# Local attention, a sine-and-cosine mixing layer and a gated layer on one core: a residual added by accumulating transfers, a shorter float64 conversion, a rounding moved to ScalarE

## The chip, the cores and the metric

The kernel runs on one core of a Trainium2 chip. The metric is the time of one execution in device microseconds (us). Besides plain times there is a profile: one execution recorded by the hardware profiler. TensorE multiplies matrices from SBUF into PSUM; VectorE (DVE) and ScalarE (ACT) do elementwise work; GpSimd (POOL) is almost unused; SyncE (SP) issues transfers. Every engine works through its own queue in order.

## The reference

Three layers follow one another on 4 batches of 768 tokens and 512 channels.

```python
# 1. local attention, 8 heads of 64: a chunk of 32 queries sees 8 memory keys,
#    16 keys to the left, its own 32 and 8 to the right
out[:, :, c0:c1] = softmax(q_c @ k_full.T / 8) @ v_full
x = out.transpose(0, 2, 1, 3).reshape(4, 768, 512)
# 2. mixing
theta = x @ w_theta
zr, zi = x * cos(theta), x * sin(theta)
u = x + einsum('ts,bsd->btd', w_tok_r, zr) + einsum('ts,bsd->btd', w_tok_i, zi)
x = u + maximum(u @ w_ch, 0)
# 3. gated layer
h = gelu_tanh(x @ w_in);  a, v = h[..., :512], h[..., 512:]
v_n = (v - mean(v)) / sqrt(var(v) + 1e-6) * g_ln
x = x + (a * (w_sg @ v_n + b_sg)) @ w_out
```

The weights w_theta, w_tok_r, w_tok_i, w_ch, w_in and w_out arrive as float64, all else as float32.

## The kernel before

Each factor of a large product is split into a rounded part `hi` and a remainder `lo`, and a product is taken as hi*hi + hi*lo + lo*hi, three matmuls where one would do.

Attention works in 24 blocks of 128 tokens (6 for each batch). Each block has four steps: `att_s` (scores, maximum, exponential), `att_t` (TensorE transposes the probabilities), `att_v` (values, division) and `att_x` (TensorE transposes the result, and `split` makes `xhi`, `xlo`). Each block loads its `q`, `ka` and `va` on SP's queue.

The mixing layer works in 48 units, one for each turn of the loop over `it`. A unit holds one block of 128 source tokens: for batch 0 all 512 channels and one half of the target tokens (12 units), for batches 1 to 3 256 channels and both halves (36 units). `theta(n)` multiplies for the angle (in turns, since 1/2pi is folded into w_theta), takes off the nearest whole number by adding and subtracting MAGIC = 1.5 * 2^23, and makes sine and cosine on ScalarE; `z_split(n)` splits x*cos and x*sin. `mix_group(n, g)` adds 6 matmuls of 128x384 into one of four accumulators in PSUM; it is called with g = 0 to 3 in each unit. In the last unit of six the accumulators are complete: two VectorE additions put xhi and xlo on top (lines 388, 389; `u` has two buffers), and SP stores 192 KB into `u_dram` (line 390). This end of four groups comes eight times. `theta` and `z_split` run two units ahead of `mix_group`.

The 4 pieces of w_theta and the 12 of w_tok are converted from float64 while the first units run. `Weights.load` brings a piece to SBUF as pairs of 32-bit words; `bits` makes the float32 with truncated mantissa from the upper word (one ScalarE pass, three VectorE passes; the third masks out the exponent); then `convert` (10 pieces of w_tok, all of w_ch and w_in) multiplies the lower word by that power of two, subtracts hi and adds: three more VectorE passes. `convert_pe` (4 pieces of w_theta, 2 of w_tok) leaves these last sums to TensorE, as three matmuls with an identity, and ScalarE copies the result. `conv_out` does the same for the 4 pieces of w_out.

After the mixing layer, `chan` takes u from `u_dram` for u + max(u @ w_ch, 0), and the gated layer follows, batch by batch.

The framework puts a semaphore wait wherever an instruction needs another's result or its buffer.

Of the kernel before, what the change touches and what calls it, by code (L numbers as in the profile page):

```python
# [6 lines left out]
F32 = mybir.dt.float32  # L7
# [13 lines left out]
NBLK = S // 128  # L21
# [11 lines left out]
def net_kernel(tc, qt, kw, vw, ident, w_theta, w_tok, w_ch, w_in, w_sg, w_out, g_ln, b_sg, out):  # L33
# [33 lines left out]
    id_th = stg.tile([128, 128], F32, name="id_th", bufs=1)  # L67
    id_r = stg.tile([128, 128], F32R, name="id_r", bufs=1)
    id_neg = stg.tile([128, 128], F32R, name="id_neg", bufs=1)
# [44 lines left out]

    class Weights:
# [28 lines left out]
        def bits(self, raw, n, scale, mag="act", rem="dve"):  # L144

            words = raw[:, 0:2 * n].rearrange("p (n t) -> p n t", t=2)
            low, high = words[:, :, 0], words[:, :, 1]
            h = self.pool.tile([128, self.n], I32, tag="cvh", name="cvh", bufs=self.ncv)[:, 0:n]
            m = self.pool.tile([128, self.n], I32, tag="cvm", name="cvm", bufs=self.ncm)[:, 0:n]
            nc.scalar.activation(  # L150
                out=h.bitcast(F32), in_=high.bitcast(F32), func=AF.Copy, scale=REBIAS
            )
            nc.vector.tensor_scalar(
                out=h, in0=h, scalar1=3, scalar2=None, op0=ALU.logical_shift_left
            )
            nc.vector.scalar_tensor_tensor(  # L156
                out=h, in0=high, scalar=-0x80000000, in1=h,
                op0=ALU.bitwise_and, op1=ALU.bitwise_or,
            )
            nc.vector.tensor_scalar(  # L160
                out=m, in0=h, scalar1=-0x800000, scalar2=None, op0=ALU.bitwise_and
            )
            return high, low, h, m

        def convert_pe(self, j, scale=None, bank=None):

            if j >= len(self.pieces):
                return
            _, hi, lo = self.pieces[j]
            raw, n, _ = self.raw.pop(j)  # L170
            one = 1.0 if scale is None else scale
            high, low, h, m = self.bits(raw, n, scale)

            w, rest = h.bitcast(F32), lo
            nc.scalar.activation(out=hi, in_=w, func=AF.Copy, scale=one)
            nc.vector.scalar_tensor_tensor(
                out=rest, in0=low.bitcast(U32), scalar=one * 2.0 ** -52, in1=m.bitcast(F32),
                op0=ALU.mult, op1=ALU.mult,
            )
            step = n if n <= 512 else n // 2  # L180
            for c in range(0, n, step):
                cv = (bank or th_tile)()[:, 0:step]
                c = slice(c, c + step)
                nc.tensor.matmul(
                    out=cv, lhsT=id_sb if scale is None else id_th, rhs=w[:, c],
                    start=True, stop=False,
                )
                nc.tensor.matmul(out=cv, lhsT=id_neg, rhs=hi[:, c], start=False, stop=False)
                nc.tensor.matmul(out=cv, lhsT=id_r, rhs=rest[:, c], start=False, stop=True)
                nc.scalar.activation(out=lo[:, c], in_=cv, func=AF.Copy)  # L190

        def convert(self, j, mag="act", rem="dve", sub="dve", add="dve"):
            if j >= len(self.pieces):
                return
            eng = {"dve": nc.vector, "pool": nc.gpsimd}
            _, hi, lo = self.pieces[j]
            raw, n, wide = self.raw.pop(j)
            if not wide:
                split(hi, lo, raw[:, 0:n].bitcast(F32), eng[sub])
                return  # L200
            high, low, h, m = self.bits(raw, n, None)
            w, rest = h.bitcast(F32), m.bitcast(F32)
            nc.scalar.activation(out=hi, in_=w, func=AF.Copy)
            nc.vector.scalar_tensor_tensor(
                out=rest, in0=low.bitcast(U32), scalar=2.0 ** -52, in1=rest,
                op0=ALU.mult, op1=ALU.mult,
            )
            eng[sub].tensor_tensor(out=w, in0=w, in1=r32(hi), op=ALU.subtract)  # L208
            eng[add].tensor_tensor(out=lo, in0=w, in1=rest, op=ALU.add)
# [69 lines left out]
    def att_x(i):  # L279
# [8 lines left out]
        split(xhi[:, :, 128 * s:128 * s + 128], xlo[:, :, 128 * s:128 * s + 128], tp3)  # L288


# [10 lines left out]
    def theta(n):  # L301
# [16 lines left out]
        else:  # L318
# [3 lines left out]
        nc.vector.tensor_scalar(  # L322
            out=t, in0=th, scalar1=MAGIC, scalar2=MAGIC, op0=ALU.add, op1=ALU.subtract
        )
# [39 lines left out]
    def mix_group(n, g):  # L364
# [18 lines left out]
        if last:  # L383
            _, xhi, xlo = sets[b % 2]
            dt = d0 + d2
            tt = slice(TC * th, TC * th + TC)
# [217 lines left out]
    def conv_out(k):  # L604
# [5 lines left out]
        nc.scalar.activation(  # L610
# [454 lines left out]
```

## Time and profile before

| | us |
|---|---|
| median of 3 runs | 746.72 |
| lowest and highest of them | 746.16 and 748.55 |
| the profiled execution | 749.29 |
| its span (first to last instruction) | 747.5 |
| TensorE busy | 723.0 |
| VectorE busy | 524.9 |
| ScalarE busy | 318.9 |
| GpSimd busy | 0.3 |

"Busy" is the time in which an engine has at least one instruction at work. Matmuls are pipelined, so a busy TensorE is not one at its peak: what it can do at best is read from the distance between the starts of matmuls that wait for nothing. Recorded durations of neighbours on one engine overlap a little. "PEclk" is the share of TensorE's full clock that was granted.

### The profile page before, as it was taken

To read this page: it belongs to the slowest core of one execution; us is meant where nothing else is said; L and a number is where in the kernel's file an instruction comes from. 1 tells how busy PE (TensorE), PEld (TensorE's weight loads), DVE (VectorE), ACT (ScalarE), POOL (GpSimd) and SP (SyncE) were. 2 spreads that over 40 slices of the span, in tenths; PEclk is the share of its full clock that TensorE was granted. 3 is DMA by queue.
4 is the path that set the end of the run, shared out by engine and by line. 5 is a ranking of instruction groups with operands and counts; after the bars stand their busy time and mean duration, and the time that the engine had idled before them with its cause. 6 is when DMAs were issued, how large, how long until landed. Compare 5 with 4: busy or idle time off the path is not lost.

```text
span 747.5 us, 16071 instructions
## 1 busy us (share of the span) xinstructions
PE 723.0 (97%) x6920; PEld 671.3 (90%) x6920; DVE 524.9 (70%) x980; ACT 318.9 (43%) x482; POOL 0.3 (0%) x6
## 2 busy tenths in 40 slices
PE   5998999999999999999999999999999999999997
PEld 2676788899999999999999998999899989998997
DVE  3999898856656575699539976977446744774375
ACT  4767553645455445463314416722342233224320
POOL 0000000000000000000000000000000000000000
PEclk9998999999999999999999999999999999999999
DMA  9575465522333331062049837002200310030002
GB/s 349 197 275 197 147 226 158 202 73 86 131 108 121 101 134 53 23 233 61 12 150 345 317 136 255 1 0 91 80 1 0 111 59 1 1 116 11 1 1 85
DMA packets 33047, 86.89 MB, mean 116 GB/s; under 512 B 3792, under 2 KB 16208, under 8 KB 32976
## 3 DMA queue, kind: packets, MB, share of 16 engines
q1 hardware_dynamic: 32976, 85.87, 33.3%
q8 instruction: 54, 0.88, 0.5%
q14 instruction: 17, 0.14, 0.1%
HBM read 66.98 MB, written 18.87 MB: 115 GB/s over the span
## 4 chain that ended last, share of the span: by engine, by line
PE 78%; DVE 14%; ACT 4%; DMA 2%; issue 1%; SPq 0%; DVEq 0%; ACTq 0%
PE acc L378 16%; PE acc L664 13%; PE acc L540 9%; PE acc L578 9%; PE acc L432 9%; PE th L311 7%; PE att L702 6%; PE att L234 3%; DVE z L336 1%; DVE cvh L156 1%; PE att L258 1%; PE att L284 1%; PE th L702 1%; PE acc L702 1%; DVE cvh L208 1%
## 5 line engine op out<-in xcount | busy, mean ns | idle before, releaser
L378 PE MATMUL acc<-tok,slot 128*128 128x384 f32 x552 | 116.8, 342 | 2.5 <-ACT slot L348 2.5
L378 PE MATMUL acc<-slot 128*128 128x384 f32 x552 | 115.5, 340 | 0.0
L378 PEld LDWEIGHTS acc<-tok,slot 128*128 128x128 f32 x552 | 94.6, 188 | 4.6 <-ACT slot L348 2.8
L378 PEld LDWEIGHTS acc<-slot 128*128 128x128 f32 x552 | 95.6, 188 | 1.7
L664 PE MATMUL acc<-sg_hi,vhi_all 128*128 128x384 f32 x192 | 64.5, 336 | 0.0
L664 PE MATMUL acc<-sg_lo,vhi_all 128*128 128x384 f32 x192 | 64.5, 336 | 0.0
L664 PE MATMUL acc<-sg_hi,vlo_all 128*128 128x384 f32 x192 | 64.3, 336 | 0.0
L311 PE MATMUL th<-th_hi,xhi 128*128 128x256 f32 (+1 forms) x168 | 52.8, 314 | 1.3 <-ACT xhi L112 1.1
L311 PE MATMUL th<-th_hi,xlo 128*128 128x256 f32 (+1 forms) x168 | 51.4, 306 | 0.6 <-DVE xlo L113 0.6
L311 PE MATMUL th<-th_lo,xhi 128*128 128x256 f32 (+1 forms) x168 | 50.6, 301 | 0.0
L112 ACT ACTIVATE gop<-gv_all 128x384 fp32r<-128x384 f32 (+1 forms) x28 | 15.9, 571 | 76.7 <-DVE gv_all L673 51.6
L669 DVE SCALAR_TENSOR_TENSOR gv_all<-acc,g_col,b_bc 128x384 f32<-128x384 f32 x32 | 19.6, 615 | 41.0 <-PE acc L664 41.0
L578 PE MATMUL acc<-x3lo,in_hi 128*128 128x384 f32 x128 | 43.1, 337 | 0.0
L578 PE MATMUL acc<-x3hi,in_hi 128*128 128x384 f32 x128 | 43.1, 337 | 0.0
L578 PE MATMUL acc<-x3hi,in_lo 128*128 128x384 f32 x128 | 43.1, 337 | 0.0
L432 PE MATMUL acc<-uhi,ch_hi 128*128 128x384 f32 x128 | 42.8, 335 | 0.0
L432 PE MATMUL acc<-ulo,ch_hi 128*128 128x384 f32 x128 | 42.8, 335 | 0.0
L432 PE MATMUL acc<-uhi,ch_lo 128*128 128x384 f32 x128 | 42.8, 334 | 0.0
L547 DVE BATCH_NORM_STATS2 bn<-gv_all 128x6 f32<-128x512 f32 x24 | 16.7, 694 | 33.7 <-ACT gv_all L546 33.6
L540 PE MATMUL acc<-in_hi,x3lo 128*128 128x512 f32 x96 | 38.0, 396 | 0.0
L540 PE MATMUL acc<-in_lo,x3hi 128*128 128x512 f32 x96 | 38.0, 396 | 0.0
L540 PE MATMUL acc<-in_hi,x3hi 128*128 128x512 f32 x96 | 38.0, 396 | 0.0
(183 smaller groups left out, 1568.7 us busy)
## 6 DMA issues: line engine op xcount, KB each, us to landing
va<-vw SPq DMA_DIRECT2D x24, 520.0 KB, 3.9
ka<-kw SPq DMA_DIRECT2D x24, 512.0 KB, 4.5
raw<-w_tok SPq DMA_DIRECT2D x12, 768.0 KB, 5.0
q<-qt SPq DMA_DIRECT2D x24, 256.0 KB, 3.2
u_dram<-u SPq DMA_DIRECT2D x32, 192.0 KB, 2.0
uf<-u_dram SPq DMA_DIRECT2D x8, 768.0 KB, 5.9
x_dram<-x2e SPq DMA_DIRECT2D x32, 192.0 KB, 3.1
x3f<-x_dram SPq DMA_DIRECT2D x8, 768.0 KB, 4.7
```

Of the source, the lines that this page charges most:

```text
L112: nc.scalar.activation(out=hi, in_=src, func=AF.Copy)
L156: nc.vector.scalar_tensor_tensor(out=h, in0=high, scalar=-0x80000000, in1=h, op0=ALU.bitwise_and, op1=ALU.bitwise_or,)
L234: nc.tensor.matmul(out=out[32 * c:32 * c + 32, j, n * a:n * a + n], lhsT=lhs[h, a, 32 * c:32 * c + 32], rhs=rhs[h, 4 * a + c, :], start=Tr ...
L311: nc.tensor.matmul(out=th, lhsT=a[:, k, tok], rhs=w[:, k, cols], start=(i == 0), stop=(i == 3 * KD - 1),)
L378: nc.tensor.matmul(out=acc[:, 0:TC], lhsT=z[ri][:, zc], rhs=w[:, ri], start=(first and i == 0), stop=(last and i == 5),)
L432: nc.tensor.matmul(out=acc[:, 0:TC], lhsT=w[:, k, ee], rhs=x[:, k, :], start=(i == 0), stop=(i == 3 * KD - 1),)
L540: nc.tensor.matmul(out=acc, lhsT=x[:, k, tt], rhs=w[:, k, :], start=(i == 0), stop=(i == 3 * KD - 1),)
L547: nc.vector.bn_stats(out=p3["bn"][s], in_=gv)
L578: nc.tensor.matmul(out=acc[:, 0:TC], lhsT=w[:, k, ff], rhs=x[:, k, :], start=(i == 0), stop=(i == 3 * KD - 1),)
L664: nc.tensor.matmul(out=acc[:, 0:TC], lhsT=v, rhs=w, start=(i == 0), stop=(i == 3 * NBLK - 1))
L669: nc.vector.scalar_tensor_tensor(out=g, in0=acc[:, 0:TC], scalar=p3["g"][:, f:f + 1], in1=p3["b"][:, tt], op0=ALU.mult, op1=ALU.add,)
L702: nc.tensor.matmul(out=bank, lhsT=wt[:, k, ee], rhs=xt[:, k, :], start=(fresh and i == 0), stop=(i == 5), skip_group_check=not fresh,)
```

## The change

1. `Weights.bits` and `convert_pe` go. A new `single` makes a float32 from the two words in three VectorE passes and two ScalarE passes: the truncated value as before, and from the lower word its top bits as an integer, which is then added to the float's bits. `convert` splits the result into hi and lo; for w_theta the remainder is one VectorE pass with the scale. The three identity tiles for TensorE go too. `conv_out` uses `single`.
2. In `theta`, ScalarE adds MAGIC while it copies the angle from PSUM, and one VectorE pass takes MAGIC and the angle off; the sign turns, so the sine's scale becomes negative.
3. When the last block of a batch has been split, the new `seed_u` stores xhi into `u_dram` (two transfers of 768 KB on SP's queue) and adds xlo there by eight accumulating transfers of 192 KB from GpSimd's queue. At the end of four groups ScalarE copies each accumulator to `u`, and an accumulating transfer from GpSimd's queue adds it to `u_dram`.

```diff
+    def single(high, low, h, r):
+        nc.scalar.activation(
+            out=h.bitcast(F32), in_=high.bitcast(F32), func=AF.Copy, scale=REBIAS
+        )
+        nc.scalar.activation(out=r, in_=low.bitcast(U32), func=AF.Copy, scale=2.0 ** -29)
+        nc.vector.tensor_scalar(
+            out=h, in0=h, scalar1=3, scalar2=None, op0=ALU.logical_shift_left
+        )
+        nc.vector.scalar_tensor_tensor(
+            out=h, in0=high, scalar=-0x80000000, in1=h, op0=ALU.bitwise_and, op1=ALU.bitwise_or
+        )
+        nc.vector.tensor_tensor(out=h, in0=h, in1=r, op=ALU.add)
+        return h.bitcast(F32)
...
-        def bits(self, raw, n, scale, mag="act", rem="dve"):
...
-        def convert_pe(self, j, scale=None, bank=None):
...
+        def convert(self, j, scale=None):
...
+            w = self.single(j, raw, n)
+            if scale is None:
+                split(hi, lo, w)
+                return
+            nc.scalar.activation(out=hi, in_=w, func=AF.Copy, scale=scale)
             nc.vector.scalar_tensor_tensor(
-                out=rest, in0=low.bitcast(U32), scalar=2.0 ** -52, in1=rest,
-                op0=ALU.mult, op1=ALU.mult,
+                out=lo, in0=w, scalar=scale, in1=r32(hi), op0=ALU.mult, op1=ALU.subtract
             )
-            eng[sub].tensor_tensor(out=w, in0=w, in1=r32(hi), op=ALU.subtract)
-            eng[add].tensor_tensor(out=lo, in0=w, in1=rest, op=ALU.add)
...
         split(xhi[:, :, 128 * s:128 * s + 128], xlo[:, :, 128 * s:128 * s + 128], tp3)
+        if s == NBLK - 1:
+            seed_u(b)
+
+    def seed_u(b):
+        _, xhi, xlo = sets[b % 2]
+        for th in range(2):
+            tt = slice(TC * th, TC * th + TC)
+            nc.sync.dma_start(out=u_dram[2 * b + th], in_=r32(xhi[:, :, tt]))
+        for th in range(2):
+            tt = slice(TC * th, TC * th + TC)
+            for k in range(KD):
+                nc.gpsimd.dma_start(
+                    out=u_dram[2 * b + th][:, k, :], in_=r32(xlo[:, k, tt]), accum_op=ALU.add
+                )
...
-        nc.vector.tensor_scalar(
-            out=t, in0=th, scalar1=MAGIC, scalar2=MAGIC, op0=ALU.add, op1=ALU.subtract
-        )
-        nc.vector.tensor_tensor(out=t, in0=th, in1=t, op=ALU.subtract)
+        nc.scalar.activation(out=t, in_=th, func=AF.Copy, bias=MAGIC)
+        nc.vector.scalar_tensor_tensor(
+            out=t, in0=t, scalar=MAGIC, in1=th, op0=ALU.subtract, op1=ALU.subtract
+        )
...
-        nc.scalar.activation(out=z[:, 1], in_=t, func=AF.Sin, scale=TWO_PI)
+        nc.scalar.activation(out=z[:, 1], in_=t, func=AF.Sin, scale=-TWO_PI)
...
-            nc.vector.tensor_tensor(out=u, in0=acc[:, 0:TC], in1=r32(xhi[:, dt, tt]), op=ALU.add)
-            (nc.gpsimd if b >= 4 else nc.vector).tensor_tensor(out=u, in0=u, in1=r32(xlo[:, dt, tt]), op=ALU.add)
-            nc.sync.dma_start(out=u_dram[2 * b + th][:, dt, :], in_=u)
+            nc.scalar.activation(out=u, in_=acc[:, 0:TC], func=AF.Copy)
+            nc.gpsimd.dma_start(out=u_dram[2 * b + th][:, dt, :], in_=u, accum_op=ALU.add)
```

## Rows read from the trace of the kernel before

**Rows 1.** Stages: length, then each engine's busy time and instructions, granted clock, DMA.

```profile
core 0: us, PE busy (x) PEld busy (x) DVE busy (x) ACT busy (x) POOL busy (x), PEclk, DMA share, GB/s
...
7.44:38.30 30.86, 27.37 (x328) 17.22 (x329) 25.43 (x45) 21.83 (x36) 0.00 (x0) 1.00 0.76 279
38.30:97.30 59.00, 52.81 (x742) 44.10 (x740) 54.27 (x86) 39.17 (x52) 0.00 (x0) 0.94 0.59 201
97.30:147.60 50.30, 47.93 (x993) 42.50 (x992) 45.48 (x82) 22.39 (x32) 0.00 (x0) 1.00 0.61 196
147.60:382.30 234.70, 232.64 (x2834) 221.99 (x2832) 156.05 (x337) 111.78 (x182) 0.00 (x0) 1.00 0.28 94
382.30:747.50 365.20, 361.05 (x1968) 344.56 (x1967) 243.69 (x432) 122.46 (x181) 0.00 (x0) 1.00 0.26 90
```

**Rows 2.** Chain that ended last, in order of time: start, length, what.

```profile
13.93 2.00 PE acc L184 x2
...
189.00 1.44 PE th L311 x12
...
203.09 1.43 PE th L311 x12
...
369.80 12.49 PE acc L378 x72
```

**Rows 3.** TensorE in order of time, `theta(0)`'s first and last matmul of 12.

```profile
24.38 0.39 PE L311 MATMUL th<-th_hi,xhi 128*128 128x512 f32 x1
...
26.94 0.39 PE L311 MATMUL th<-th_hi,xlo 128*128 128x512 f32 x1
```

**Rows 4.** VectorE's groups until 150 us, shapes apart: count, busy, mean ns, idle before.

```profile
L204 DVE SCALAR_TENSOR_TENSOR cvm<-raw,cvm 128x768 f32<-128x768 uint32 x10 | 9.5, 952 | 0.0
...
L160 DVE TENSOR_SCALAR cvm<-cvh 128x768 int32<-128x768 int32 x12 | 6.6, 551 | 0.1
...
L209 DVE TENSOR_TENSOR slot<-cvh,cvm 128x768 fp32r<-128x768 f32 x6 | 5.7, 953 | 0.1
...
L388 DVE TENSOR_TENSOR u<-acc,xhi 128x384 f32<-128x384 f32 x8 | 4.4, 552 | 0.6 <-DMA u_dram<-u 0.6
...
L322 DVE TENSOR_SCALAR t<-th 128x512 f32<-128x512 f32 x6 | 4.1, 680 | 1.4 <-PE th L311 1.2
```

**Rows 5.** ScalarE's groups until 150 us, the same columns.

```profile
L150 ACT ACTIVATE cvh<-raw 128x768 f32<-128x768 f32 x12 | 10.9, 908 | 6.5 <-DVE slot L209 4.5 <-DVE tok L209 1.9
...
L190 ACT ACTIVATE th_lo<-acc 128x512 fp32r<-128x512 f32 x4 | 2.4, 596 | 4.0 <-PE acc L189 4.0
L190 ACT ACTIVATE tok<-acc 128x384 fp32r<-128x384 f32 x4 | 1.8, 486 | 0.4 <-PE acc L189 0.4
```

**Rows 6.** VectorE in order of time around the last block of batch 0.

```profile
81.33 0.69 DVE L113 TENSOR_TENSOR xlo<-att,xhi 128x512 fp32r<-128x512 f32 x1
...
94.92 0.56 DVE L388 TENSOR_TENSOR u<-acc,xhi 128x384 f32<-128x384 f32 x1
```

**Rows 7.** Transfers by line: count, KB each, median us from issue to landing.

```profile
q<-qt SPq DMA_DIRECT2D x24, 256.0 KB, 3.2
u_dram<-u SPq DMA_DIRECT2D x32, 192.0 KB, 2.0
uf<-u_dram SPq DMA_DIRECT2D x8, 768.0 KB, 5.9
```

**Rows 8.** TensorE in order of time, end of four groups in a steady unit.

```profile
298.17 1.21 PE L378 MATMUL acc<-slot 128*128 128x384 f32 x6
...
307.26 1.20 PE L378 MATMUL acc<-tok,slot 128*128 128x384 f32 x6
```

**Rows 9.** Waits, whole span, engines' and SP queue's: us in total, times, longest.

```profile
DVE u L388 <- DMA u_dram<-u: 2.6, 4, 0.9
...
SPq L390 <- DVE u L389: 105.1, 20, 27.1
```

**Rows 10.** SP queue in order of time: issue of one load.

```profile
99.44 0.33 SPq L219 DMA_DIRECT2D q<-qt  x1
```

More of the change, by code (lines that the diff above doesn't have):

```diff
@@ L142, in load, with single @@
             self.raw[j] = raw, n, wide
[L144 removed]
+        def single(self, j, raw, n):
             words = raw[:, 0:2 * n].rearrange("p (n t) -> p n t", t=2)
@@ L148, in bits @@
             h = self.pool.tile([128, self.n], I32, tag="cvh", name="cvh", bufs=self.ncv)[:, 0:n]
-            m = self.pool.tile([128, self.n], I32, tag="cvm", name="cvm", bufs=self.ncm)[:, 0:n]
-            nc.scalar.activation(
-                out=h.bitcast(F32), in_=high.bitcast(F32), func=AF.Copy, scale=REBIAS
-            )
-            nc.vector.tensor_scalar(
[L154 to L163, printed above, removed]
-        def convert_pe(self, j, scale=None, bank=None):
+            r = self.pool.tile([128, self.n], I32, tag="cvm", name="cvm", bufs=self.ncm)[:, 0:n]
+            return single(high, low, h, r)
+        def convert(self, j, scale=None):
             if j >= len(self.pieces):
@@ L169, in convert_pe @@
             _, hi, lo = self.pieces[j]
[L170 to L177, printed above, removed]
-                op0=ALU.mult, op1=ALU.mult,
-            )
@@ L180, in convert_pe @@
[L180 to L196, printed above, removed]
             raw, n, wide = self.raw.pop(j)
             if not wide:
-                split(hi, lo, raw[:, 0:n].bitcast(F32), eng[sub])
+                split(hi, lo, raw[:, 0:n].bitcast(F32))
                 return
-            high, low, h, m = self.bits(raw, n, None)
-            w, rest = h.bitcast(F32), m.bitcast(F32)
-            nc.scalar.activation(out=hi, in_=w, func=AF.Copy)
+            w = self.single(j, raw, n)
@@ L609, in conv_out @@
         m = p3["stm"][:, DM * k:DM * k + DM]
-        nc.scalar.activation(
-            out=h.bitcast(F32), in_=high.bitcast(F32), func=AF.Copy, scale=REBIAS
-        )
-        nc.vector.tensor_scalar(
-            out=h, in0=h, scalar1=3, scalar2=None, op0=ALU.logical_shift_left
-        )
-        nc.vector.scalar_tensor_tensor(
-            out=h, in0=high, scalar=-0x80000000, in1=h, op0=ALU.bitwise_and, op1=ALU.bitwise_or
-        )
-        nc.vector.tensor_scalar(
-            out=m, in0=h, scalar1=-0x800000, scalar2=None, op0=ALU.bitwise_and
-        )
-        rest, w = m.bitcast(F32), h.bitcast(F32)
-        nc.vector.scalar_tensor_tensor(
-            out=rest, in0=low.bitcast(U32), scalar=2.0 ** -52, in1=rest,
-            op0=ALU.mult, op1=ALU.mult,
-        )
-        nc.vector.tensor_tensor(out=w, in0=w, in1=rest, op=ALU.add)
+        w = single(high, low, h, m)
         hi, lo = p3["ow"]
@@ L817, in net_kernel @@
         w1s.load(5)
-        nc.scalar.activation(out=id_th, in_=id_sb, func=AF.Copy, scale=1.0 / TWO_PI)
-        nc.scalar.activation(out=id_r, in_=id_sb, func=AF.Copy)
-        nc.scalar.activation(out=id_neg, in_=id_sb, func=AF.Copy, scale=-1.0)
         def th_conv():
             nonlocal jw
-            w1s.convert_pe(jw, scale=1.0 / TWO_PI, bank=acc_tile)
+            w1s.convert(jw, scale=1.0 / TWO_PI)
             jw += 1
@@ L830, in tok_conv @@
                 place(jw - NTH - NBLK)
-            if jw < NTH + 2:
-                w1s.convert_pe(jw, bank=acc_tile)
-            else:
-                w1s.convert(jw)
+            w1s.convert(jw)
             w1s.load(jw + 2)
```

7 lines of the change are left out of this document (removed).

## The prediction

> **What bounds the kernel now.** I read the busy times by stage first. From 147.6 us on TensorE is busy for 232.6 of 234.7 us and then for 361.1 of 365.2, with VectorE at two thirds [rows 1]. That TensorE is not only busy but at its pace there, the chain shows: 72 matmuls of 128x384 take 12.49 us, 0.1735 us each, with nothing between them, and two units with one attention block repeat every 203.09 - 189.00 = 14.09 us [rows 2]. So nothing that VectorE or ScalarE saves after 147.6 us shortens the run; it can only be lengthened there.
>
> Before 147.6 us it is otherwise. VectorE is busy for 25.4 of 30.9 us, for 54.3 of 59.0 and for 45.5 of 50.3 [rows 1], over 90% in the last two, and its groups have next to no idle time ahead of them [rows 4]. TensorE's busy time looks as high, but much less than that is needed. In 38.3 to 97.3 us it has six units of 24 matmuls (25.0 us), four thetas of 12 matmuls, each 26.94 - 24.38 = 2.56 us over 11 distances, so 2.79 us (11.2) [rows 3], and four attention blocks. A block costs 14.09 - 2 x 4.16 - 2 x 1.43 = 2.9 us [rows 2], so 11.6. Together 47.8 of 59.0 us. In 97.3 to 147.6 us it has six units (25.0), three thetas of 1.43 (4.3) and, in the program's order, six blocks, three of them without their last step, which I put at 5.6 blocks (16.2): 45.5 of 50.3 us. The most that these two stages can give is 11.2 + 4.8 = 16.0 us.
>
> **Part 1, the conversion.** For each of the 10 w_tok pieces of `convert`, six VectorE passes become four: the mask (0.551) and one pass of 0.952 go; the integer addition and the subtraction take the places of the other two, and I price them as the passes they resemble [rows 4]. An integer addition was not seen before; the nearest row, a 128x768 pass with two inputs, is 0.953, and no such pass in the rows is dearer, so 0.95 with a range of 0.55 to 1.9 (one pass, or two). Saved: 10 x 1.50 = 15.0 us of VectorE, six pieces of it in the earlier stage and four in the later. ScalarE gains one strided pass of 0.908 a piece [rows 5]: 9.1 us.
>
> The six pieces of `convert_pe` are no gain for VectorE: mask and one multiply go, addition and remainder come, about +0.3 to +0.4 each, +2 us. But TensorE loses its identity matmuls, which stand on the chain (two of them take 2.00 us [rows 2]), and ScalarE's copy of their sum (0.596 and 2 x 0.486) is replaced by the new strided pass [rows 5], about even. In 7.4 to 38.3 us VectorE has 30.9 - 25.4 = 5.4 us of gaps [rows 1], partly waits behind those matmuls. I take 2 us of them as gained, with 0 and 5 as bounds; without these matmuls TensorE is also idler there, and the granted clock, which is full (2.4 GHz) or half (1.2), already comes to a mean of 0.94 in the next stage [rows 1], which is why I don't take more. w_ch, w_in and w_out save VectorE time only where TensorE sets the pace: nothing.
>
> **Part 2, the rounding.** VectorE loses a pass of 0.680 for each 512-wide theta [rows 4] (less for the 256-wide ones); the remaining pass reads the same operands as before. ScalarE gains a copy from PSUM, 0.596 by its nearest row [rows 5]. The angle now crosses engines once more. From batch 1 on that is covered by theta running two units ahead, 14.09 us with a block between them [rows 2]; were the cover gone it would be about 0.6 us a theta.
>
> The Trainium skill (ScalarE: Activation LUTs, Rules for kernel authors) says to keep additions on VectorE rather than ScalarE. The trace does not bear it out for operands in PSUM: a 128x384 copy on ScalarE is 0.486 and a 128x384 VectorE pass 0.552 [rows 4, 5]. By the rule this part would cost time, by the rows it moves work off the fuller engine.
>
> **Part 3, the residual.** At each of eight ends of four groups VectorE loses 2 x 0.552 for each group [rows 4]: 8.8 us in the two ends before 147.6 us. ScalarE gains 0.486 a group [rows 5]. SP's queue loses stores in front of which it stood for 105 us in all [rows 9]; what stood behind them were loads of q and ka, and they now go earlier. Against that stand new waits. `u` has two buffers, so the third copy waits until the first accumulation has landed, and ScalarE stands in order: theta's rounding, sine and the next split stand behind it, and TensorE's next accumulator. A plain store lands in 2.0 us, a load of 256 KB from HBM in 3.2 [rows 7]. The accumulation reads its destination and writes it, so 2.0 + 3.2, about 5 us; bounds 2 and 10 (twice that). In a steady unit the first group's matmuls have been issued at 298.17 and the accumulator of the third is taken again at 307.26 [rows 8]: 9.1 us. Two copies of 0.49 and the issue (0.33 on SP [rows 10]) leave 7.7 us for the landing. At 5 us TensorE sees nothing; VectorE waited 2.6 us in all for these buffers before [rows 9].
>
> The seed must be there first. In batch 0, from the last block's xlo (82.0) to the first use of an accumulator (94.9) are 12.9 us [rows 6]. The seed is like a 768 KB load, 5.9 us [rows 7]; then GpSimd issues eight transfers at 0.33 to 1 us (2.6 to 8) and its own queue is in order. So 8.5 to 14: just in time or a little late. For this and ScalarE's waits in the two early ends I take a loss of 1.5 us, 0 to 9.
>
> **The sum.** Earlier stage: VectorE 54.3 - 9.0 (six pieces) - 3.4 (five thetas) - 1.7 (three additions to u) = 40.2 us; ScalarE 39.2 + 5.4 (six pieces) + 3.0 (five thetas) + 1.0 (two copies to u) - 1.0 (the two copies of L190 that fall in it) = 47.6; TensorE 47.8. All wait for one another, so the stage comes to some 52.5 instead of 59.0: -6.5. Later stage: VectorE 45.5 - 6.0 (four pieces) - 1.0 (narrow thetas, an estimate from the wide) - 7.2 (13 additions) = 31.3; ScalarE 22.4 + 3.6 + 1.2 + 6 x 0.49 = 30.1; TensorE 45.5. That is the mix of the steady stage (VectorE two thirds, TensorE 99%), so 46.5 instead of 50.3: -3.8. With -2 before and +1.5 for the new waits: -10.8 us on the profiled 749.3 (span 747.5 and 1.8 around it), 738.5. That execution lay 2.6 us over the runs' median of 746.7, so the forecast for the median is 736 us.
>
> **The rivals.**
>
> *Accumulations land late* (slower). Were landing 10 us, TensorE would lose 10 - 7.7 = 2.3 us at each of eight ends, 18.4 us: 736 + 18 = 754. It decides from 7.7 + 10.8 / 8 = 9.1 us on. For it: nothing in the trace has run this path, GpSimd being idle [rows 1]. Against it: every transfer of up to 768 KB lands within 5.9 us in the median [rows 7] and the DMA share is 0.28 there [rows 1]. The Trainium skill (SBUF — State Buffer, Who interferes with whom) has a reason for lateness: descriptors that GpSimd writes wait while VectorE runs a two-port pass, such as a shift over SBUF. No run here shows it; such passes are 0.55 us long and shorter than the slack above [rows 4].
>
> *ScalarE becomes the bound* (little gain). In 38.3 to 97.3 us it is left with 47.6 of what would be 52.5 us. If its present gaps (59.0 - 39.2 = 19.8 us) stay, being waits for work that comes no earlier, that stage gives nothing and the first 30 us nothing: 749.3 - 3.8 + 1.5 = 747.0, median 744. For it: the chain of the angle gets longer, and ScalarE's queue is in order. Against it: the gaps are waits for others' results, and VectorE, which gives most of them, has 14 us less to do.
>
> *All slack goes* (more gain): 16.0 + 5 = 21 us, median 726. Against it: with VectorE alone as full as two engines would then be, TensorE keeps 45.5 of 50.3 us, nine tenths.
>
> *The seed is late*: at 2 us for each of GpSimd's issues, 5.9 + 16 = 22 us against 12.9 in batch 0: a loss of 9 instead of 1.5, median 743.5.
>
> **How the numbers follow.** Forecast 0.55 (own range 730 to 742), ScalarE the bound 0.13, seed late 0.08, all slack 0.08, accumulations late 0.16. Two and a bit microseconds, 0.3%, is what a measurement of this kernel can tell from none: 744.5 and 749 are the limits. Faster: 0.55 + 0.08 + 0.05 of the seed + 0.05 of ScalarE, 0.73; same 0.11; slower 0.16. The range leaves out the late accumulations and a little below: 725 to 749.
>
> **What would show it.** Right: the first unit of batch 1 starts 9 to 13 us before 147.6; the masks, the identity matmuls and lines 388 and 389 are gone; VectorE is below 80% of the stages before; the accumulations land within 7 us and no wait of ScalarE's u copy is long enough to reach TensorE; the time from there to the end is unchanged at 600 us. Wrong: TensorE idle at the eight ends behind copies of u, or ScalarE over 90% busy with TensorE waiting for it before batch 1.

## The result, and the profile after

The changed kernel takes 754.13 us (median of 12 runs, 750.43 to 760.62), the kernel before in the same comparison 747.11 (745.62 to 749.82): a ratio of 1.0101, 95% interval 1.0075 to 1.0127. It is slower by 1%; 736 was forecast, with 725 to 749 as range, so the time lies outside the range and on the other side of no change. The profiled execution took 755.3 us, its span is 753.5.

The stages of the kernel after, cut where its own units start (first unit 33.83, seventh 91.16, first of batch 1 138.62, `chan` 385.86); columns as in [rows 1]:

```profile
7.44:33.83 26.39, 16.61 (x297) 12.00 (x297) 24.69 (x42) 22.98 (x34) 0.00 (x0) 0.87 0.88 343
33.83:91.16 57.33, 52.45 (x738) 43.95 (x736) 45.30 (x69) 46.30 (x64) 8.43 (x10) 0.94 0.82 251
91.16:138.62 47.46, 44.87 (x909) 39.06 (x909) 29.96 (x53) 25.33 (x40) 3.62 (x5) 1.00 0.67 193
138.62:385.86 247.24, 238.75 (x2920) 225.71 (x2918) 121.25 (x247) 136.92 (x250) 42.57 (x49) 1.00 0.54 130
385.86:753.50 367.64, 361.79 (x1969) 344.70 (x1968) 230.89 (x404) 129.49 (x195) 1.73 (x2) 1.00 0.27 89
```

The first matmul of batch 1 stands right behind the four transposes that read `slot_x`. TensorE there, first before, then after:

```profile
141.98 0.60 PE L284 MATMUL att<-id_sb,slot_x 128*128 128x128 f32 x4
142.33 1.31 PE L378 MATMUL acc<-tok,slot 128*128 128x384 f32 x6
```

```profile
138.27 0.60 PE L254 MATMUL att<-id_sb,slot_x 128*128 128x128 f32 x4
138.62 0.77 PE L362 MATMUL acc<-tok,slot 128*128 128x384 f32 x3
```

So before, the unit began at 142.33 us, not at the 147.6 that I had taken from the chain. Cut there, the two stages of before that answer to the third and fourth of after are:

```profile
97.30:142.33 45.03, 43.24 (x907) 38.62 (x906) 41.04 (x75) 19.86 (x28) 0.00 (x0) 1.00 0.60 194
142.33:382.13 239.80, 237.16 (x2920) 225.70 (x2919) 160.49 (x345) 114.30 (x185) 0.00 (x0) 1.00 0.29 96
```

Stage by stage, after less before: to the first unit 33.83 - 38.32 = -4.5 us; the next stage 57.3 - 59.0 = -1.7; the next 47.5 - 45.0 = +2.4; batches 1 to 3 of the mixing 247.2 - 239.8 = +7.4; from `chan` on 367.6 - 365.4 = +2.3. Sum +6.0, the difference of the spans (753.5 - 747.5). The two stages from which 10.3 us were forecast give nothing together (-1.7 + 2.4). In batches 1 to 3 TensorE's busy time is nearly the same (238.75 and 237.16), but its idle time grew from 2.6 to 8.5 us.

VectorE is lighter (452.8 us busy for 524.9), ScalarE fuller (362.4 for 318.9), and GpSimd issues accumulating transfers for 56 us. The new rows: GpSimd's issue, and transfers with the median time to landing:

```profile
L271 POOL DMA_DIRECT2D u_dram<-xlo x32 | 28.3, 1031 | 131.0 <-DMA u_dram<-xhi 70.8 <-issue 24.4 <-DVE t L307 15.6
L371 POOL DMA_DIRECT2D u_dram<-u x32 | 28.0, 926 | 204.4 <-ACT u L370 200.1 <-ACT slot_x L306 3.8 <-issue 0.5
```

```profile
u_dram<-xhi SPq DMA_DIRECT2D x8, 768.0 KB, 5.5
u_dram<-xlo POOLq DMA_DIRECT2D x32, 192.0 KB, 5.5
u_dram<-u POOLq DMA_DIRECT2D x32, 192.0 KB, 5.3
```

An accumulation lands after 5.3 us in the median (3.5 to 8.3), near the 5 of the forecast. Yet ScalarE waits for it (waits over the whole span: total, times, longest):

```profile
ACT u L370 <- DMA u_dram<-u: 35.1, 12, 5.4
```

ScalarE, GpSimd and TensorE in order of time at one end of four groups show what that wait does:

```profile
225.60 0.85 ACT L370 ACTIVATE u<-acc 128x384 f32<-128x384 f32 x2
...
226.48 1.78 POOL L371 DMA_DIRECT2D u_dram<-u  x2 [25.96 <-ACT u L370]
...
231.26 0.49 ACT L370 ACTIVATE u<-acc 128x384 f32<-128x384 f32 x1 [4.18 <-DMA u_dram<-u]
231.65 0.59 ACT L109 ACTIVATE xhi<-att 128x512 fp32r<-128x512 f32 x1
...
232.61 0.38 ACT L306 ACTIVATE slot_x<-th 128x256 f32<-128x256 f32 x1
...
235.76 1.28 ACT L221 ACT_TABLE_LOAD   x1
237.10 0.63 ACT L221 ACTIVATE p<-p 128x512 f32<-128x512 f32 x1
...
237.78 0.66 PE L228 MATMUL att<-id_sb,p 128*128 128x128 f32 x4 [1.20 <-ACT p L221]
```

Two copies go at once; the third stands 4.18 us until the first accumulation has freed its buffer. Behind it on ScalarE stand the split of x, the rounding of the next angle, the sines, and the exponential of the attention block, and TensorE waits for that exponential, not for an accumulator. The same wait of TensorE comes at 194.14 (1.48 us) and 282.63 (2.13). At another end, 323.33, it does wait for an accumulator that a late copy holds. TensorE's waits in batches 1 to 3 (138.62 to 385.86; total, times, longest; all of them 8.4 us, before 2.5):

```profile
PE att L228 <- ACT p L221: 4.8, 3, 2.1
PE acc L362 <- ACT u L370: 1.7, 1, 1.7
PE th L295 <- DVE slot_x L307: 1.6, 2, 1.4
```

The Trainium skill (PSUM — Partial Sum Buffer, Engine vs sequencer instructions) says that ScalarE's queue is strictly first in, first out; the trace agrees: all that stands behind the copy waits out its 4.18 us too.

### The profile page after: what moved, and what is told of

Read it like the earlier page. It is cut to its first block, busy times and chain, and to the rows that moved or that the text cites. A ratio compares the mean times of both kernels' runs of the same rounds, so it can differ in the third digit from the quotient of the medians.

```text
span 753.5 us, 16049 instructions
## 1 busy us (share of the span) xinstructions
PE 715.6 (95%) x6888; PEld 666.4 (88%) x6888; DVE 452.8 (60%) x814; ACT 362.4 (48%) x581; POOL 56.7 (8%) x70
## 4 chain that ended last, share of the span: by engine, by line
PE 55%; issue 21%; DMA 9%; DVE 6%; ACT 6%; POOL 3%; SPq 0%; POOLq 0%; ACTq 0%; DVEq 0%
PE acc L628 13%; PE acc L521 9%; PE acc L559 9%; PE acc L413 7%; PE att L666 6%; DMA u_dram<-u 4%; PE acc L362 4%; PE th L295 3%; DMA raw<-w_ch 3%; POOL u_dram L271 2%; DMA u_dram<-xhi 1%; PE th L666 1%; PE acc L666 1%; POOL u_dram L371 1%; PE att L204 1%
## 5 line engine op out<-in xcount | busy, mean ns | idle before, releaser
L295 PE MATMUL th<-th_hi,xhi 128*128 128x256 f32 (+1 forms) x168 | 54.5, 325 | 5.0 <-ACT xhi L109 3.1
L371 POOL DMA_DIRECT2D u_dram<-u x32 | 28.0, 926 | 204.4 <-ACT u L370 200.1
L295 PEld LDWEIGHTS th<-th_hi,xhi 128*128 128x128 f32 x168 | 32.9, 196 | 10.3 <-ACT xhi L109 6.2
L307 DVE SCALAR_TENSOR_TENSOR slot_x<-slot_x,th 128x256 f32<-128x256 f32 x34 | 14.3, 420 | 40.3 <-ACT slot_x L306 40.3
L271 POOL DMA_DIRECT2D u_dram<-xlo x32 | 28.3, 1031 | 131.0 <-DMA u_dram<-xhi 70.8
```

The source lines that it names most:

```text
L271: nc.gpsimd.dma_start(out=u_dram[2 * b + th][:, k, :], in_=r32(xlo[:, k, tt]), accum_op=ALU.add)
L295: nc.tensor.matmul(out=th, lhsT=a[:, k, tok], rhs=w[:, k, cols], start=(i == 0), stop=(i == 3 * KD - 1),)
L307: nc.vector.scalar_tensor_tensor(out=t, in0=t, scalar=MAGIC, in1=th, op0=ALU.subtract, op1=ALU.subtract)
L371: nc.gpsimd.dma_start(out=u_dram[2 * b + th][:, dt, :], in_=u, accum_op=ALU.add)
```

## Experiments

Each kernel was compared with the kernel before on the same chip, in five rounds. All ratios are to that. Kernels 3, 14, 15 and 18 ran 6 times, kernel 7 5 times, kernel 9 7 times, the others 12.

| kernel | us | before | ratio, 95% interval |
|---|---|---|---|
| 1 conversion alone | 746.80 | 747.39 | 1.0005, 0.9989 to 1.0021 |
| 2 rounding alone | 747.54 | 747.39 | 1.0001, 0.9985 to 1.0018 |
| 3 residual alone | 758.12 | 747.39 | 1.0155, 1.0128 to 1.0183 |
| 4 changed, residual as before | 746.37 | 747.39 | 0.9986, 0.9968 to 1.0005 |
| 5 four buffers, two raw of w_ch | 747.00 | 746.58 | 1.0003, 0.9991 to 1.0015 |
| 6 accumulation in batch 0 only | 745.93 | 746.58 | 0.9986, 0.9975 to 0.9997 |
| 7 copy on VectorE | 759.42 | 746.58 | 1.0158, 1.0131 to 1.0185 |
| 8 plain stores of `u` | 745.54 | 746.58 | 0.9984, 0.9970 to 0.9999 |
| 9 as 6, filling matmuls | 752.31 | 747.87 | 1.0049, 1.0028 to 1.0070 |
| 10 as 5, batches 0 to 2 | 749.09 | 747.87 | 1.0016, 1.0001 to 1.0032 |
| 11 as 10, filling matmuls | 750.46 | 747.87 | 1.0046, 1.0032 to 1.0061 |
| 12 four buffers, w_ch untouched | 747.04 | 746.62 | 0.9999, 0.9987 to 1.0010 |
| 13 as 12, batches 0 to 2 | 746.59 | 746.62 | 1.0004, 0.9991 to 1.0018 |
| 14 as 6, identity matmuls | 749.43 | 746.62 | 1.0036, 1.0022 to 1.0051 |
| 15 as 13, identity matmuls | 751.19 | 746.62 | 1.0064, 1.0045 to 1.0082 |
| 16 before, less for TensorE | 748.00 | 747.73 | 1.0004, 0.9988 to 1.0019 |
| 17 as 6, less for TensorE | 746.37 | 747.73 | 0.9974, 0.9955 to 0.9993 |
| 18 as 6, less for VectorE | 752.83 | 747.73 | 1.0075, 1.0052 to 1.0098 |

### Which part costs

Kernels 1 to 3 make one part of the change in the kernel before; kernel 4 takes part 3 out of the changed one:

```diff
...
-            nc.scalar.activation(out=u, in_=acc[:, 0:TC], func=AF.Copy)
-            nc.gpsimd.dma_start(out=u_dram[2 * b + th][:, dt, :], in_=u, accum_op=ALU.add)
+            nc.vector.tensor_tensor(out=u, in0=acc[:, 0:TC], in1=r32(xhi[:, dt, tt]), op=ALU.add)
+            ...
+            nc.sync.dma_start(out=u_dram[2 * b + th][:, dt, :], in_=u)
```

> The kernel before with the conversion alone changed (float32 by an integer addition). Theory Q (ScalarE's queue: the loss comes from the copy to u, which waits in ScalarE's order for the accumulating transfer of two groups earlier): the conversion carries most of the 9.0 us that the first unit of batch 1 comes earlier and loses nothing later, so 6 to 9 us under before, 738 to 741. Rival C (ScalarE's added copies, conversion and rounding, make its other work late): the later conversions of w_ch, w_in and w_out give some of it back, 742 to 748.

> The kernel before with the rounding of the angle alone moved to ScalarE. Theory Q: 3.4 us of VectorE saved before batch 1, of which 1 to 3 us show, nothing later: 744 to 746. Rival C: the angle goes once more through ScalarE's queue in each of the later units, 0.3 to 0.6 us for each of some 20 thetas: 750 to 759.

> The kernel before with the residual alone by accumulating transfers. Theory Q: a small gain ahead of batch 1 (up to 3 us) and about 15 us lost at the ends of four groups and in the first x2 of the next part: 757 to 763, slower by 1.3 to 2.1%. Rival C: the loss is not here, 743 to 748.

> The changed kernel with the residual as before: VectorE adds and SP stores. Theory Q: the gain of the start stays but for what VectorE's additions cost in it (first unit of batch 1 6 to 9 us before 147.6), and the 15 us behind it are gone: 737 to 741. Rival C: the start is early all the same and it is lost later as in the changed kernel: 750 to 756.

The residual alone costs 1.55%, more than the whole change; the loss is there. Kernels 2, 3 and 4 lie outside rival C's ranges (only kernel 1 lies in one), and rival C falls. But the two other parts give next to nothing: 746.8, 747.5, and together 746.4, where theory Q had 738 to 741, 744 to 746 and 737 to 741. Half of theory Q failed as well. The transposes ahead of batch 1 stand at 138.88 us in kernel 1, 139.17 in kernel 2, 139.27 in kernel 4 and 140.03 in kernel 3, for 141.98 before and 138.27 in the changed kernel, so each part alone seems to bring 2 to 3 us and all together 3.7. But this lead is there already at the first unit, and not all of it comes from the change: up to that unit kernel 3 has the instructions of the kernel before, in the same order on TensorE, VectorE and ScalarE, and starts it 3.3 us earlier all the same. The first unit before, then in kernel 3:

```profile
38.32 1.04 PE L378 MATMUL acc<-tok,slot 128*128 128x384 f32 x5
```

```profile
34.99 1.04 PE L392 MATMUL acc<-tok,slot 128*128 128x384 f32 x5
```

From the first unit to these transposes the kernel before takes 103.7 us, kernels 1 to 4 take 105.0, 102.3, 105.0 and 104.4, and the changed kernel 104.4. One execution each, but none gains more than 1.3 us there, although VectorE has less to do in all of them: something else than VectorE's work holds that stretch.

### Two buffers and a queue in order

Kernel 5 and kernel 12 give `u` four buffers. In kernel 5 room comes from w_ch's raw buffers; in kernel 12 the third and fourth copy of an end use the tile of `t`, free by then, and one of two `t_slots`:

```diff
-    NRAW, NRAW3 = 3, 2
+    NRAW, NRAW3 = 2, 2
...
-            u = wk.tile([128, TC], F32, tag="u", name="u", bufs=2)
+            u = wk.tile([128, TC], F32, tag="u", name="u", bufs=4)
```

```diff
...
-            u = wk.tile([128, TC], F32, tag="u", name="u", bufs=2)
+            if b == 0 or g < 2:
+                u = wk.tile([128, TC], F32, tag="u", name="u", bufs=2)
+            elif g == 2:
+                u = wk.tile([128, 512], F32, tag="t", name="t", bufs=1)[:, 0:TC]
+            else:
+                u = t_slots[1][:, 0:TC]
```

> The changed kernel with four buffers of u for two (room for them by two in place of three raw buffers of w_ch). All four copies of an end can be made before the first accumulation has landed. Theory Q: no wait of ScalarE for u, TensorE waits for no exponential at the ends of groups, the 9.0 us of the start stay: 738 to 743. Rival T (the accumulating transfers themselves, their traffic and GpSimd's issues, are the price): still 751 to 756.

> The changed kernel with four buffers of u from batch 1 on, without touching w_ch: the third copy of an end goes into the buffer of t, which is free by then, the fourth into one of the two t_slots, whose four halves become two. Theory Q (two buffers of u are the whole loss): last transposes some 7 us before those of the kernel before, and from there to chan nothing lost: chan starts at 375 to 377, 739 to 742. Rival W2 (the seed of the last batch stands before loads on SP, and ScalarE waits for these): still 3 us lost near 323 us, 744 to 747.

In kernel 12 ScalarE waits for no accumulation at the ends from batch 1 on. Between the transposes ahead of batch 1 and the last ones, kernel 12, after and before (in this order) show:

```profile
138.30:310.60 172.30, 172.00 (x2509) 161.52 (x2508) 86.52 (x172) 105.85 (x176) 32.14 (x37) 1.00 0.61 143
```

```profile
138.30:316.50 178.20, 173.03 (x2510) 161.62 (x2509) 86.56 (x172) 104.58 (x175) 32.11 (x37) 1.00 0.57 138
```

```profile
142.00:317.00 175.00, 172.49 (x2510) 161.34 (x2508) 112.08 (x230) 89.76 (x136) 0.00 (x0) 1.00 0.30 98
```

The same 2,510 matmuls, the same transfers and seeds as after, and TensorE idle for 0.3 us in place of 5.2: the accumulating transfers cost nothing there once their wait stands in front of nothing, and the stage is even 2.7 us shorter than before. So the wait for two buffers is 5.9 us of this stage, and kernel 12 as a whole is level with before, 7 us under the changed kernel. Theory Q holds for the loss, rival T falls. It fails for the rest: 747.0 in both kernels and not 738 to 743 or 739 to 742. Between the last transposes and `chan` kernel 12 loses 2.6 us again (67.7 for 65.1), nearly the 3 of rival W2; the next section comes back to that.

Kernel 7 moves the copy to VectorE, kernel 8 makes GpSimd's transfers of `u` plain stores. Its expectation speaks of all of GpSimd's transfers into `u_dram`; the edit leaves those of the seed (xlo) accumulating:

```diff
-            nc.scalar.activation(out=u, in_=acc[:, 0:TC], func=AF.Copy)
+            nc.vector.tensor_copy(out=u, in_=acc[:, 0:TC])
```

```diff
-            nc.gpsimd.dma_start(out=u_dram[2 * b + th][:, dt, :], in_=u, accum_op=ALU.add)
+            nc.gpsimd.dma_start(out=u_dram[2 * b + th][:, dt, :], in_=u)
```

> The changed kernel with the copy from the accumulator to u on VectorE in place of ScalarE, two buffers as there. Theory Q: the wait for the buffer is the same 4 us and moves to VectorE, behind which stand the maximum, the splits and the products: TensorE waits for those instead of the exponential, 748 to 756. Rival S (only ScalarE's order matters, VectorE has room): 738 to 744.

> The changed kernel with all of GpSimd's transfers into u_dram made plain stores: same queue, same number and issue, nothing read back; the residual is left out of the computation. Theory Q: they land in 2 to 3 us for 5.3, so ScalarE's waits shrink from 4 us to 1 or 2 and most of the loss goes: 740 to 746. Rival T as GpSimd's issue or its queue: 751 to 756.

Kernel 7, 759.4, is above its theory's upper bound, and rival S falls: VectorE now waits (first row), the splits stand behind it, and TensorE waits up to 2.91 us for one of them at 145.61 (second).

```profile
DVE u L370 <- DMA u_dram<-u: 25.2, 13, 3.5
```

```profile
145.61 0.38 PE L295 MATMUL th<-th_hi,xlo 128*128 128x256 f32 x1 [2.91 <-DVE xlo L110]
```

In kernel 8 the stores land in 3.4 us, ScalarE waits 16.1 us for 35.1, and the loss is gone with less than 2 us of landing; TensorE's three waits for the exponential are 0.94, 0.82 and 0.71 us. GpSimd's issue, which it keeps, was not the price.

```profile
u_dram<-u POOLq DMA_DIRECT2D x32, 192.0 KB, 3.4
```

```profile
ACT u L370 <- DMA u_dram<-u: 16.1, 13, 3.3
```

### Batches

Kernel 6 accumulates in batch 0 only (`if b == 0` around the two lines of part 3 and around the seed, else the lines of before), kernels 10 and 13 in batches 0 to 2.

> The changed kernel with the accumulating transfers in batch 0 alone; from batch 1 on VectorE adds and SP stores as before. Theory Q: the early start of batch 1 (about 138.6 us) is kept and nothing is lost behind it: 737 to 742. Rival E (the early start is not worth what it seems, TensorE has to make up the work later): 745 to 748, as without any of the residual's change.

> The changed kernel with four buffers of u and the accumulating transfers in batches 0 to 2 only; the last batch adds on VectorE and is stored by SP as before. With four buffers in all batches the last transposes came 6.9 us before those of the kernel before (310.1 to 317.0), and 3.4 us of that went between 318 and 330 us, where ScalarE stood for loads of w_ch and u, queued on SP behind the last batch's seed. Theory Q, with that seed as the place: the loss goes, 740 to 743. Rival W (two raw buffers of w_ch in place of three make the loads late, seed or no seed): 745 to 748.

> The same four buffers, accumulating transfers in batches 0 to 2 only, the last batch as before. Theory Q: 739 to 742. Rival W (the loss near 323 us came from two raw buffers of w_ch) gives the same here; if the loss near 323 us stays at 3 us or more, neither the seed nor w_ch's buffers made it: 745 to 748.

Kernels 4 and 6 are the best versions that compute everything, 0.14% under before by the ratio, at the edge of what can be told. For kernel 6 rival E has it: the early start is worth 1 us at most. Kernels 10 and 13 lose 6 to 7 us of profile between the last transposes and `chan` (kernel 13: 311.5 to 383.4 us, before 317.0 to 382.1), in that batch without a seed and, in kernel 13, with all raw buffers; rivals W and W2 both fall. (Kernel 13's profiled execution, 750.7, is the slowest of its 12; its median is 746.6.) Kernel 13's ScalarE and TensorE:

```profile
317.67 0.43 ACT L114 ACTIVATE cvh<-raw 128x256 f32<-128x256 f32 x1 [4.97 <-DMA raw<-w_ch]
318.01 0.37 ACT L307 ACTIVATE slot_x<-th 128x256 f32<-128x256 f32 x1
```

```profile
318.88 0.39 PE L295 MATMUL th<-th_hi,xhi 128*128 128x256 f32 x1 [1.22 <-DVE slot_x L308]
...
327.45 0.58 PE L295 MATMUL th<-th_hi,xhi 128*128 128x256 f32 x1 [2.71 <-DVE slot_x L308]
```

The rounding that part 2 moved to ScalarE stands behind w_ch's conversion, which waits for its load; before, VectorE did the rounding, and ScalarE's longest wait for w_ch was 0.8 us. The loads are not issued later in kernel 13 but earlier, the first at 311.12 us for 320.02 before; they take longer to land, 7.2 us in the median of eight for 2.9. Accumulating transfers are in flight at that time; that they are the reason isn't shown.

The idle time is only half of the loss. From 311.5 us to `chan` TensorE is idle for 3.9 us, in the kernel before, from 317.0 us on, for 0.1, and it is busy 3.0 us longer for the same matmuls (68.0 and 65.0): the granted clock is 0.50 from 326.8 to 333.6 us, from the second of these waits on, where the kernel before has 1.00. Kernel 10 is the same, with 0.51 from 324.8 to 331.7 us; in kernel 12, with waits of at most 1.00 us there, the clock stays at 1.00.

### What holds the start

Kernels 9 and 11 put eight matmuls that nobody reads where TensorE stands idle in the first 45 us; 14 and 15 give back the identity matmuls of the first six pieces.

```diff
+        if i < 2:
+            for _ in range(3):
+                nc.tensor.matmul(
+                    out=acc_tile(), lhsT=id_sb, rhs=pt.rearrange("p a t -> p (a t)"),
+                    start=True, stop=True,
+                )
...
+        if i == 2:
+            for _ in range(2):
+                nc.tensor.matmul(
+                    out=acc_tile()[:, 0:384], lhsT=id_sb, rhs=x[s][:, 0:384],
...
```

```diff
...
-            w1s.convert(jw, scale=1.0 / TWO_PI)
+            w1s.convert_pe(jw, scale=1.0 / TWO_PI, bank=acc_tile)
...
```

> The kernel with accumulation in batch 0 alone, and eight matmuls more that nobody reads, put where TensorE stands idle in the first 45 us: three of 128x512 behind the att_v of each of the first two attention blocks, two of 128x384 behind the transposes of the third. Theory K (clock): in that kernel the granted clock is 0.50 in 28 to 32 us and 0.63 in 44 to 48, each time after a stretch in which TensorE is mostly idle, where the kernel before has 1.00; with the fillers it stays at 1.00 and the first units come 2 to 4 us earlier: 741 to 744. Rival L (ScalarE and VectorE in turn set the pace there, whatever the clock): the clock is at 1.00 and the time is as without fillers, 745 to 747.

> Both edits: accumulation in batches 0 to 2 with four buffers, and the eight filling matmuls of the start. If theory K and theory Q both hold: 737 to 741. If only one of them: 741 to 744. If neither: 745 to 748.

> The kernel with accumulation in batch 0 alone, and the first six pieces converted by identity matmuls as in the kernel before; rounding, integer addition in the other pieces and the residual of batch 0 stay changed. Theory K (clock): the granted clock stays at 1.00 to 50 us, and what the first unit loses by the longer conversion (0 to 3 us) is got back by 90 us: 743 to 746. Rival L (clock of no weight there): the first unit starts 3 to 4 us later and stays so, 747 to 750.

> The identity matmuls for the first six pieces, four buffers of u, accumulation in batches 0 to 2. Theory Q with theory K: 737 to 741. Q alone: 742 to 745. Neither: 747 to 750.

The granted clock in the changed kernel sinks to half (1.2 GHz) twice, behind stretches in which TensorE was busy for 1.02 and 2.01 of 4 us; before, it is 1.00 in these stretches and sinks once, to 0.50 at 60 to 64 us:

```profile
24.00:28.00 4.00, 1.02 (x6) 0.73 (x6) 3.23 (x6) 3.97 (x6) 0.00 (x0) 0.73 0.81 323
28.00:32.00 4.00, 3.98 (x71) 2.81 (x71) 4.00 (x6) 3.72 (x6) 0.00 (x0) 0.50 0.32 91
40.00:44.00 4.00, 2.01 (x69) 1.64 (x70) 2.73 (x5) 4.00 (x7) 0.00 (x0) 0.87 0.99 372
44.00:48.00 4.00, 4.00 (x72) 2.67 (x71) 3.78 (x6) 3.85 (x5) 0.00 (x0) 0.50 0.62 214
```

Kernel 14 keeps the clock at 1.00 to 100 us, kernel 9 only to 38 us; there it is 0.50 up to 44 us, and the first unit comes at 42.83 us for 34.03 in kernel 6, so the filling matmuls did not do what they were put in for. Both kernels are slower than kernel 6: kernel 14 lies in rival L's range, kernel 9 above both ranges, and kernels 11 and 15, with the same edits, four buffers and accumulation in batches 0 to 2, above all of theirs. Theory K is not borne out by them. But they don't refute it either, for another loss is in them: the order that the framework makes differs, and at the end of batch 0's first half the exponential falls behind a waiting copy of `u` (kernel 9: TensorE waits 4.02 us at 99.30) or TensorE waits for the copy itself (kernel 14: 4.18 at 101.61). With each of these waits the granted clock goes to 0.50 again (kernel 9: 99.4 to 102.8 us, kernel 14: 100.2 to 107.0). Kernels 16 to 18 take work away:

```diff
+        np_ = 2 if b == 0 and g > 1 else 3
...
-            for z, w in ((zhi, whi), (zhi, wlo), (zlo, whi)):
+            for z, w in ((zhi, whi), (zhi, wlo), (zlo, whi))[:np_]:
...
```

```diff
-        nc.scalar.activation(out=r, in_=low.bitcast(U32), func=AF.Copy, scale=2.0 ** -29)
...
-        nc.vector.tensor_tensor(out=h, in0=h, in1=r, op=ALU.add)
```

> The kernel before with four matmuls fewer in each of the 12 units of batch 0 (of the groups 2 and 3 the product of the small part of z with the large part of w_tok is left out of the computation): 12 x 4 x 0.1735 = 8.3 us of TensorE, 4.2 us of it from 97 us on. Theory V (the forecast's: VectorE sets the pace up to 147.6 us): 0 to 1.5 us gained, 745 to 747. Rival T (from some 70 us on TensorE's own work sets it): the 4.2 us of the six units from 97 us on and 1 to 2 of those before are gained, 740 to 743.

> The same four matmuls fewer in each unit of batch 0, in the kernel with accumulating transfers in batch 0 alone (745.9). Theory V: VectorE has become lighter, so TensorE is nearer to the pace and 3 to 5 us are gained: 741 to 743. Rival T: 5 to 7 us, 739 to 741. If the chain of the angle through ScalarE and VectorE holds the stage whatever TensorE has to do: 744 to 746.

> The kernel with accumulating transfers in batch 0 alone, without the low words in the conversion (no ScalarE pass for them and no integer addition; the low part is left out of the computation): for the 16 pieces of the start one pass each of VectorE and ScalarE, 0.55 to 0.95 us, 10 us or more of both. Theory V: if these two engines still set the pace before 100 us, 4 to 6 us are gained, 740 to 742. Rival T: under 1.5 us, 744.5 to 746.

Kernel 16 stays level with before, as theory V had it. Its profile shows more. From the seventh unit to the transposes ahead of batch 1 TensorE goes from 97.33 to 141.98 before and from 98.64 to 140.24 in kernel 16 (the first line is of the kernel before):

```profile
97.33 1.12 PE L378 MATMUL acc<-slot 128*128 128x384 f32 x5
```

```profile
98.64 1.12 PE L379 MATMUL acc<-slot 128*128 128x384 f32 x5
...
140.24 0.66 PE L284 MATMUL att<-id_sb,slot_x 128*128 128x128 f32 x4
```

That is 41.6 us for 44.7: of the 4.2 us taken away in these six units 3.1 are gained. Kernel 17 against kernel 6 says the same, 90.61 to 133.85 for 90.13 to 137.46: 43.2 us for 47.3, and 4.1 are gained. So from the seventh unit on TensorE's own work sets the pace, as rival T had it.

Between the first and the seventh unit it doesn't. There kernel 17 takes 55.7 us and kernel 6 56.1, although 4.2 us of TensorE's work are gone here too, and kernel 18, with 3.7 us less of VectorE and 2.7 less of ScalarE in this stage, takes 58.1 (mean granted clock 0.97 in all three). Neither TensorE's work alone nor that of the other two sets the pace of this stage. In kernel 16 the gain is given back in it: 61.9 us for 59.0 before, with a mean granted clock of 0.89 for 0.94.

Kernel 18 is the surprise: with less to do it is 0.9% slower than kernel 6. Kernel 18 and then kernel 6, ScalarE and TensorE at the end of batch 0's first half:

```profile
95.96 0.49 ACT L371 ACTIVATE u<-acc 128x384 f32<-128x384 f32 x1 [3.65 <-DMA u_dram<-u]
96.47 1.28 ACT L219 ACT_TABLE_LOAD   x1
97.76 0.63 ACT L219 ACTIVATE p<-p 128x512 f32<-128x512 f32 x1
...
98.44 0.66 PE L226 MATMUL att<-id_sb,p 128*128 128x128 f32 x4 [3.54 <-ACT p L219]
```

```profile
91.69 0.63 ACT L221 ACTIVATE p<-p 128x512 f32<-128x512 f32 x1
92.38 0.66 PE L228 MATMUL att<-id_sb,p 128*128 128x128 f32 x4 [0.32 <-ACT p L221]
94.33 0.49 ACT L373 ACTIVATE u<-acc 128x384 f32<-128x384 f32 x1 [2.01 <-DMA u_dram<-u]
```

The waits of the copy are alike, 3.65 and 2.01 us. In kernel 6 the exponential goes first and TensorE loses 0.32 us, in kernel 18 it goes behind and TensorE loses 3.54. The price of such a wait is set by what stands behind it. These 3.2 us are half of the 6.6 between the two profiles; behind the wait the granted clock is 0.50 besides (99.9 to 103.3 us, in kernel 6 1.00). The other half stands ahead of the seventh unit and isn't explained.

Kernel 17 shows the clock's weight better than the kernels made for it. The same program ran 12 times: three executions with a mean granted clock of 0.992 to 0.993 took 741.1 to 742.0 us, nine with 0.982 to 0.989 took 745.1 to 747.2. The means differ by 0.0063 of the clock, 4.7 us of 745, and by 4.9 us of time. The changed kernel's own 12 go the same way in the main, from 750.43 at 0.994 to 760.62 at 0.985 (one, 753.83, has 0.995). The runs of the kernel before that were compared with kernels 1 to 18 lie at 0.994 or 0.995, all of them, and still spread from 744.7 to 750.8 us. Kernel 17's gain on kernel 6 appears in the executions that keep the clock, and is lost with it in the others; its median alone would have spoken for neither theory, and stands next to the third reading, a chain of the angle. Which comes first, the lower clock or a wait that leaves TensorE idle, these means don't show.

## Why the prediction was wrong

- **The whole**: -10.8 us forecast, +6.0 in the spans. Of the 16.8 us between them the new waits are 8.2, the later stage 6.2, the earlier 4.8; the first 30 us came out 2.5 better.
- **The first 30 us**: -2 forecast, -4.5 measured, inside its bounds (0 to 5), and the masks and identity matmuls are gone as said. That they bring the 4.5 isn't shown: kernel 3 keeps them and its first unit comes 3.3 us earlier than before, too. To be inside the bounds may be luck.
- **Earlier stage**: -6.5 forecast, -1.7 measured. ScalarE's busy time came out close (46.3 for 47.6), VectorE's 5.1 too high (45.3 for 40.2: it fell by 9.0 where passes of 14.1 were taken off), and the length 57.3 for 52.5. The step that failed is "all wait for one another, so the stage comes to some 52.5": it takes the stage to be as long as its fullest engines need, and kernels 17 and 18 show that less work for TensorE, or for VectorE and ScalarE, does not shorten it. That the chain of the angle through the three holds it, as the rival *ScalarE becomes the bound* had it in kind, would fit and isn't shown. The clock takes part; how much of the 4.8 us is its, the runs don't settle.
- **Later stage**: -3.8 forecast, +2.4 measured. The step that failed is "45.5 of 50.3", the slack of TensorE. The stage was cut at the wrong place: the piece of the chain at 147.63 is not the unit's first, which began at 142.33. Up to there the prediction's own prices make six units 25.0, two thetas 2.9 and 5.5 blocks 16.0, 43.9 of 45.0 us: TensorE was at its pace, with 1.1 us to give and not 4.8, and kernels 16 and 17 show that it was. By the same cut the sign "the first unit of batch 1 starts 9 to 13 us before 147.6" came true by luck: 138.62 is 9.0 before 147.6, but 3.7 before the true start, and that lead is older than the stage. That the stage grew by 2.4 is not explained; in kernel 4 the chain there holds a load of w_tok for 6.5 us.
- **New waits**: +1.5 forecast with bounds 0 and 9; +9.7 measured from batch 1 on (7.4 + 2.3), of which four buffers take away 9.2 in the profiles (753.5 - 744.3) and 7 in the medians. The step that failed is "At 5 us TensorE sees nothing". The landing, 5.3, and the budget of 7.7 us (7.8 by its own terms) were right, but the budget was that of the accumulator's next use [rows 8]. ScalarE's queue had a shorter one: the exponential, in order behind the copy. I had named theta's rounding, sine and the split as what stands behind it, and not the exponential. Of TensorE's 8.4 us of waits in batches 1 to 3 the exponential has 4.8, an accumulator 1.7, the angle's rounding 1.6.
- **Rivals**: *Accumulations land late* gave 754 and the measured time is 754.1, but by another mechanism; the landing was not late. *The seed is late* was not seen in the changed kernel: TensorE waited 0.24 us at batch 0's first end. Its account let the whole seed wait for the last block; in the trace the store of its first half goes out at 51.82 us, ahead of the last block's transposes at 75.38.
- **Medians**: the profiled execution of before lay 2.2 us above its median in the comparison (749.3 and 747.1). Kernel 12's lay 0.9 below its own, kernel 13's 4.1 above. The 3.2 us that kernel 12's profile gains on before are therefore no gain in the medians; a difference of two single executions is good to some 3 us here.

Left open: what paces the stage from the first to the seventh unit once VectorE is lighter, what the clock takes there, and why the loads of w_ch take longer to land.

## What to carry to other kernels

A wait is priced by what stands behind it on its engine, not by when its own buffer or accumulator is needed next: list all instructions behind it until the wait would end and find the first that the full engine needs. Before work is put on a less busy engine, ask which of its present results are due at once; an exponential in an attention chain is. To count what a stage can give, cut it at the first instruction of the next unit on the engine's own timeline, and count what else falls in the cut. Before a lead in one profile is put down to a change, look for the same lead in a kernel whose work up to there is unchanged: here that was 3.3 of 4.5 us.

## What the runs showed of the hardware

- An accumulating transfer of 192 KB into HBM landed in 5.3 us in the median, a plain store from the same queue in 3.4 (kernel 8), from SP's in 2.0 [rows 7]; GpSimd was busy 0.93 to 1.03 us with the issue of each, SP 0.33 with that of a load [rows 10].
- The integer addition of float bits (128x768, recorded as 128x1536 uint16) took 0.951 us in the mean of 12, the 0.95 assumed; a 128x512 strided ScalarE pass over the lower words 0.66, a 128x768 one 0.91.
- Less work for TensorE where it isn't the limit went with a lower granted clock, though the ranges touch. The mean over a run is 0.993 to 1.000 in kernels 2, 3, 14 and 15, which keep the identity matmuls, 0.981 to 0.995 in all kernels without them, and 0.985 to 0.993 in kernel 16, which keeps them and drops others. Among executions of one program 0.0063 of it went with 4.9 us.
- With waits of TensorE of 2.71 us (kernel 13), 3.54 (18), 4.02 (9) and 4.18 (14) the granted clock went to 0.50, so that the matmuls behind the wait took longer as well (in kernel 13 by 3.0 us).
